# Score maxima in nine units of 512 keys in place of twelve of 384

## The chip, the cores and the metric

The kernel runs on one core of a Trainium2 chip. That core has a matrix engine (TensorE, PE in the profile, with its weight loads listed apart as PEld), a vector engine (VectorE, DVE), a scalar engine (ScalarE, ACT), GpSimd (POOL) and SyncE (SP), which issues the transfers here. The metric is the device time of one execution in microseconds, median of three runs.

## The reference

Attention over pooled queries, and behind it a feed-forward layer with g = h − tanh(h) in the middle:

```python
q_pool = q.reshape(B, H, S // 2, 2, D).mean(axis=3)          # B=8, H=8, S=1152, D=64
scores = np.matmul(q_pool, k.transpose(0, 1, 3, 2)) / np.sqrt(D)
scores = scores - np.max(scores, axis=-1, keepdims=True)
attn = np.exp(scores)
attn = attn / (np.sum(attn, axis=-1, keepdims=True) + 1e-09)
x = np.matmul(attn, v)            # then laid out as 4608 tokens x 512
h = x @ w_in                      # 512 x 2048
out = (h - np.tanh(h)) @ w_out    # 2048 x 512
```

All of it is float32. Each head has 576 pooled queries and 1152 keys. The part that the change touches is `np.max(scores, axis=-1)`.

## The kernel before

Two heads form a pair and lie in the two halves of the 128 partitions (64 rows each), so that two matmuls with 64 rows of contraction, one for each head, run side by side. There are 32 pairs. For each pair the program makes these stages, in this order on PE:

- **Scores.** 18 places, two halves of the queries (288 each) by nine tiles of 128 keys. At each place (`scores`) PE makes a transposed score tile of both heads, keys on partitions, by four pairs of matmuls of 288 columns: high by high part, high by low, low by high, and a row of maxima (`m_row` with `sel`) that subtracts each query's maximum. ACT takes the exponential out of the PSUM buffer into a tile `p`, and POOL adds the `p` tiles up for the sums.
- **P·V.** 18 places again; at each PE multiplies one `p` tile with `v` (float32). When a half is done ACT copies the result out (`pv_out`).
- **Sums** of the exponentials, by matmuls with ones, and ACT copies them out (`s_s`).

The maxima are wanted per query before a pair's scores begin, so they are computed one pair ahead. `max_part(pi, i)` is one step of this: it takes a PSUM buffer, PE writes untransposed scores (queries on partitions) of the high parts of `q` and `k` of both heads into it, and DVE reduces them to one maximum per query and head (`mx`). The 576 queries are four tiles of 128 and a last one of 64; the two heads' last tiles share one operand, `q_last`. Steps 0 to 11 are four tiles by three thirds of the keys (CH = 384), steps 12 and 13 the last tile. `max_row` then combines the three partial maxima of each query (`nm`), transposes them and sends them through DRAM (`m_dram`) into the row `m_row`.

Where a step stands is written out by hand. A table `at` holds, for each pair and place, what is to be done behind that place's scores or P·V step. Every engine is wrapped so that its instructions keep the order in which the program names them. For the pair after the current one, steps 0 to 11 stand behind places 1, 2, 4, 5, 7, 8, 10, 11, 13, 14, 16 and 17 of the scores, `max_row` behind place 17; steps 12 and 13 of a pair stand two pairs ahead, behind the sums. DVE has other work in the P·V stage: the query sums (`raw`), the low parts (`kq_l`) and, in most pairs, a quarter of it at a time, the conversion of the feed-forward weights (tiles `w_t`, `w_hl`).

All these users of PSUM share one ring of four buffers of two banks each:

```python
ring = new("ring", 4, space=PSUM)
def psum():
    return ring.tile([P, 2, 512], F32, name="ps")
```

A buffer is handed out in the order of the calls: score, maximum step, P·V result and sums alike. Whoever takes a buffer waits until the fourth call before it has been read out, by ACT (scores, `o_s`, `s_s`) or by DVE (maxima). Head 0 writes the first bank of a buffer, head 1 the second.

After the last pair the feed-forward stage follows, from about 825 us on, in its own PSUM buffers.

The profile gives nearly all instructions the line of the helper that keeps the order (L37), so they are told apart by tiles: `mx<-ps` is a maximum's reduction, `ps<-kq_h` with 384 columns its matmul, with 288 columns the first of a score's four pairs.

Of the kernel before, what the change touches and what calls it, by code (L numbers as in the profile page):

```python
# [12 lines left out]
ALU = mybir.AluOpType  # L13
AX = mybir.AxisListType
# [32 lines left out]
def attention_ffn_kernel(  # L47
# [16 lines left out]
    P = 128  # L64
    B, NP, _, _, SQ = q.shape
    S = k.shape[-1]
# [4 lines left out]
    CH = S // 3  # L71
# [5 lines left out]
    pe, act, dve, pool, sp = (InOrder(tc, e) for e in (nc.tensor, nc.scalar, nc.vector, nc.gpsimd, nc.sync))  # L77
# [32 lines left out]
    class X:  # L110
# [25 lines left out]
        def high(self, c):  # L136
            act.activation(self.h[:, c], self.r[c], AF.Copy)

        def low(self, eng, c):
            eng.tensor_tensor(self.l[:, c], self.r[c], self.h[:, c].bitcast(F32), op=ALU.subtract)  # L140
# [14 lines left out]
    with ExitStack() as actx:  # L155
# [6 lines left out]
        op = new("op", 2)  # L162
# [17 lines left out]
        def rows(t, h):  # L180
            return t[h * D:h * D + D]

        def psum():
            return ring.tile([P, 2, 512], F32, name="ps")
# [42 lines left out]
            sp.dma_start(w.v, v[w.b, w.hp])  # L227


        order = [(t, c) for t in range(4) for c in range(3)] + [(4, 0), (4, 2)]  # L230

        def max_part(pi, i):

            w = pairs[pi]
            t, c = order[i]
            q0 = t * P
            ps = psum()
            if t < 4:
                for h in range(2):
                    pe.matmul(ps[:, h, 0:CH], rows(w.hi, h)[:, q0:q0 + P], rows(w.hi, h)[:, SQ + c * CH:SQ + (c + 1) * CH],  # L240
                              start=True, stop=True)
                dve.tensor_reduce(w.mx[:, t, c], ps[:, :, 0:CH], axis=AX.X, op=ALU.max)
            else:
                n = min(2, 3 - c)
                for a in range(n):
                    pe.matmul(ps[:, a, 0:CH], q_last[pi % 2], w.hi[:, SQ + (c + a) * CH:SQ + (c + a + 1) * CH],
                              start=True, stop=True)
                dve.tensor_reduce(w.mx[:, 4, c // 2, 0:n], ps[:, 0:n, 0:CH], axis=AX.X, op=ALU.max)
# [147 lines left out]
        def add(pi, place, f, *args):  # L396
            at.setdefault((pi, place), []).append(lambda: f(*args))

        for pi in range(1, n_pair):
            for i in range(12):  # L400
                add(pi - 1, i // 2 * 3 + 1 + i % 2, max_part, pi, i)
            if pi >= 2:
                for i in range(12, 14):
                    add(pi - 2, 2 * NS, max_part, pi, i)
            add(pi - 1, NS - 1, max_row, pi)
        for pi in range(n_pair):
# [36 lines left out]
        load_v(0)  # L443
        query_sums(0)
        high(0, 2)
        for i in range(9):
            max_part(0, i)
        max_row(0, 0, 3)
        low(0)
        for i in range(9, 14):  # L450
            max_part(0, i)
        max_row(0, 3, 4)
        query_sums(1)
        high(1)
        for i in range(12, 14):
            max_part(1, i)
        blocks[0].load()

# [4 lines left out]
        for pi in range(n_pair):  # L463
            w = pairs[pi]
            ps = [Half(), Half()]
# [101 lines left out]
    for ci in range(len(chunks)):  # L567
        c = Chunk()
# [8 lines left out]
        for f in range(NF):  # L577
            n = ci * NF + f
# [71 lines left out]
```

## Time and profile before

| | |
|---|---|
| time, median of 3 runs | 1634.74 us (1633.24 to 1636.42) |
| the profiled execution's own time | 1633.7 us |
| its span | 1631.9 us |
| mean granted TensorE clock | 0.996 |
| PE busy | 1586.2 us, 97% of the span |
| DVE busy | 1280.5 us, 78% |
| ACT busy | 938.5 us, 58% |
| first and last maximum reduction start | 8.0 and 793.8 us |

A group row gives line, engine, operation, output and input tiles with shapes and the number of instructions; behind the bar the time that they were busy, the mean duration of one in ns, then the idle time of the engine ahead of them and who ended it. A timeline row gives start and length in us, then the same names; instructions of one kind that follow each other are merged into a row ("x2"), and in brackets stands the idle time before and what ended it. A window row gives the stretch and its length, then busy time and count of PE, PEld, DVE, ACT and POOL, the granted clock, the share of the DMA engines and GB/s. The chain of waits goes back from the last instruction to what released each one.

### The profile page before, as it was taken

The numbers are of one execution on the slowest core, as the hardware profiler recorded it, in microseconds if no ns is written. First come the engines' busy times: TensorE is split into PE (matmuls) and PEld (weight loads), VectorE is DVE, ScalarE is ACT, GpSimd is POOL, SyncE is SP. The second block draws the span as 40 slices with busy tenths as digits, with TensorE's granted clock in tenths as the row PEclk, the third lists the DMA queues.
The fourth block names the chain that finished last, engine by engine and source line by source line (L and its number), as shares of the span: only waits on it lengthen the run. The fifth ranks groups of instructions, "written<-read, shape, count | busy, mean of one in ns | idle before, by whom it ended". The sixth has DMA issues, their size and how long they took to land.

```text
span 1631.9 us, 30673 instructions
## 1 busy us (share of the span) xinstructions
PE 1586.2 (97%) x12012; PEld 1228.4 (75%) x12012; DVE 1280.5 (78%) x1621; ACT 938.5 (58%) x1584; POOL 1113.3 (68%) x749
## 2 busy tenths in 40 slices
PE   5999999999999999999999999999999999999998
PEld 4777676776776776777768888888888888888886
DVE  6788888898889898969447777777777777777776
ACT  3565565565655656656535656555555656555554
POOL 3777786776767767778756666666757675666654
PEclk9999999999999999999999999999999999999999
DMA  4335444344453554333471101001010101020000
GB/s 169 107 119 197 167 150 182 133 183 162 155 214 135 200 182 160 131 123 100 152 310 34 65 7 48 31 7 65 13 65 14 65 14 65 13 65 10 30 1 26
DMA packets 79602, 166.15 MB, mean 102 GB/s; under 512 B 11874, under 2 KB 38498, under 8 KB 77410
## 3 DMA queue, kind: packets, MB, share of 16 engines
q1 hardware_dynamic: 79458, 164.20, 28.3%
q8 instruction: 94, 1.54, 0.4%
q14 instruction: 50, 0.41, 0.1%
HBM read 126.12 MB, written 38.04 MB: 101 GB/s over the span
## 4 chain that ended last, share of the span: by engine, by line
PE 83%; DVE 11%; DMA 2%; issue 2%; ACT 2%; POOL 0%; SPq 0%; POOLq 0%; DVEq 0%; ACTq 0%
PE ps L37 35%; PE ps_h L37 24%; PE ps_o L37 24%; DVE mx L37 3%; DVE w_t L37 3%; DVE kq_l L37 1%; DVE w_hl L37 1%; DMA wi_dram<-w_hl 1%; DVE raw L37 1%; ACT w_t L37 1%; DMA m_dram<-tr 0%; SPq L37 0%; DMA q<-in_q_dram 0%; ACT q_last L37 0%; POOL sum L37 0%
## 5 line engine op out<-in xcount | busy, mean ns | idle before, releaser
L37 DVE TENSOR_REDUCE mx<-ps 128x2 f32<-128x768 f32 x448 | 396.6, 924 | 86.9 <-PE ps L37 85.0
L37 POOL TENSOR_TENSOR sum<-p,p 128x576 f32<-128x576 f32 x192 | 300.6, 1566 | 196.7 <-ACT p L37 196.5
L37 ACT ACTIVATE p<-ps 128x576 f32<-128x576 f32 x576 | 353.2, 653 | 112.1 <-PE ps L37 93.7
L37 POOL TENSOR_SCALAR g_m<-g_u 128x512 uint8<-128x512 f32 (+1 forms) x145 | 250.6, 1728 | 197.6 <-ACT g_u L37 182.5
L37 POOL TENSOR_TENSOR sum<-sum,p 128x576 f32<-128x576 f32 x192 | 301.1, 1568 | 29.2 <-ACT p L37 15.1
L37 PE MATMUL ps<-kq_h 64*128 64x288 f32 (+1 forms) x1920 | 289.3, 345 | 28.0 <-DVE mx L37 17.6
L37 PE MATMUL ps<-p,v 128*64 128x288 f32 x2304 | 286.4, 407 | 0.1
L37 DVE SCALAR_TENSOR_TENSOR ps_w<-g_u,ps_h 128x512 f32<-128x512 f32 (+1 forms) x145 | 100.4, 693 | 191.3 <-ACT g_t L37 191.2
L37 PEld LDWEIGHTS ps<-p,v 128*64 128x64 f32 x2304 | 162.6, 137 | 114.4 <-ACT p L37 6.9
L37 POOL TENSOR_TENSOR g_lo<-g_s,g_hi 128x512 fp32r<-128x512 f32 (+1 forms) x145 | 186.6, 1287 | 89.5 <-ACT g_hi L37 89.5
L37 PE MATMUL ps_o<-w,g_hi 128*128 128x512 f32 x792 | 244.5, 390 | 1.0 <-ACT g_hi L37 1.0
L37 PEld LDWEIGHTS ps<-kq_h 64*128 64x128 f32 x1920 | 181.3, 187 | 80.8 <-DVE mx L37 33.0
L37 ACT ACTIVATE g_u<-ps_h 128x512 f32<-128x512 f32 (+1 forms) x145 | 85.8, 591 | 244.0 <-PE ps_h L37 242.3
L37 PE MATMUL ps_h<-x_h,w 128*128 128x512 f32 (+1 forms) x800 | 214.8, 390 | 0.0
L37 ACT ACTIVATE g_s<-g_u,pc 128x512 f32<-128x512 f32 x290 | 193.2, 714 | 11.3
L37 PEld LDWEIGHTS ps_h<-x_h,w 128*128 128x128 f32 x800 | 149.6, 188 | 32.4
L37 PEld LDWEIGHTS ps_o<-w,g_hi 128*128 128x128 f32 x792 | 148.5, 188 | 33.6 <-ACT g_hi L37 1.4
L37 PE MATMUL ps<-kq_l,kq_h 64*128 64x288 f32 x1152 | 171.8, 295 | 0.0
L37 PE MATMUL ps<-kq_h,kq_l 64*128 64x288 f32 x1152 | 171.5, 294 | 0.0
L37 PE MATMUL ps<-m_row,sel 64*128 64x288 f32 x1152 | 171.2, 293 | 0.0
L37 PE MATMUL ps_o<-w,g_lo 128*128 128x512 f32 x396 | 154.8, 391 | 0.6 <-POOL g_lo L37 0.5
L37 DVE COPY_PREDICATED g_s<-g_m,g_t 128x512 f32<-128x512 uint8 (+1 forms) x145 | 108.4, 748 | 15.0
(92 smaller groups left out, 2368.3 us busy)
## 6 DMA issues: line engine op xcount, KB each, us to landing
raw<-in_k_dram SPq DMA_DIRECT2D x32, 576.0 KB
q<-in_q_dram SPq DMA_DIRECT2D x32, 576.0 KB
v<-in_v_dram SPq DMA_DIRECT2D x32, 576.0 KB
x_dram<-o_s SPq DMA_DIRECT2D x32, 288.0 KB
x_l<-x_dram SPq DMA_DIRECT2D x9, 1024.0 KB
out_dram<-o_f SPq DMA_DIRECT2D x36, 256.0 KB
w_raw<-in_w_in_dram SPq DMA_DIRECT2D x8, 1024.0 KB
w_off<-in_w_in_dram SPq DMA_DIRECT2D x8, 1024.0 KB
```

The lines of the kernel that those rows point to most:

```text
L37: i = f(*args, **kwargs)
```

## The change

The four full query tiles have 4 × 1152 = 4608 columns of keys. They are cut into nine units of 512 columns that run on from one tile into the next. Units 0, 1, 3, 5, 7 and 8 lie in one tile; unit 2 has 128 columns of tile 0 and 384 of tile 1, unit 4 256 and 256 of tiles 1 and 2, unit 6 384 and 128 of tiles 2 and 3. A unit takes one buffer of the ring and fills both its banks. A unit in one tile has two matmuls of 512 columns (one a head) and one reduction of 2 × 512 elements; one that crosses has four matmuls and two reductions. Each tile still gets three partial maxima. The units stand behind the places 1, 3, 5, ... 17; the last tile's two steps keep their place, behind the sums two pairs ahead. In the opening, ahead of pair 0, seven units stand where nine steps stood ahead of the first `max_row`.

```diff
@@ -227,20 +227,38 @@
             sp.dma_start(w.v, v[w.b, w.hp])
 
 
-        order = [(t, c) for t in range(4) for c in range(3)] + [(4, 0), (4, 2)]
+
+
+        units, n_part = [], {}
+        for u in range(0, 4 * S, 512):
+            units.append([])
+            left = 512
+            while left:
+                t, k0 = divmod(u, S)
+                n = min(S - k0, left)
+                units[-1].append((t, n_part.setdefault(t, 0), k0, n))
+                n_part[t] += 1
+                u, left = u + n, left - n
+        assert set(n_part.values()) == {3}
+        NU = len(units)
 
         def max_part(pi, i):
 
             w = pairs[pi]
-            t, c = order[i]
-            q0 = t * P
             ps = psum()
-            if t < 4:
-                for h in range(2):
-                    pe.matmul(ps[:, h, 0:CH], rows(w.hi, h)[:, q0:q0 + P], rows(w.hi, h)[:, SQ + c * CH:SQ + (c + 1) * CH],
-                              start=True, stop=True)
-                dve.tensor_reduce(w.mx[:, t, c], ps[:, :, 0:CH], axis=AX.X, op=ALU.max)
+            if i < NU:
+                at_ = 0
+                for t, c, k0, n in units[i]:
+                    for h in range(2):
+                        pe.matmul(ps[:, h, at_:at_ + n], rows(w.hi, h)[:, t * P:(t + 1) * P], rows(w.hi, h)[:, SQ + k0:SQ + k0 + n],
+                                  start=True, stop=True)
+                    at_ += n
+                at_ = 0
+                for t, c, k0, n in units[i]:
+                    dve.tensor_reduce(w.mx[:, t, c], ps[:, :, at_:at_ + n], axis=AX.X, op=ALU.max)
+                    at_ += n
             else:
+                c = 2 * (i - NU)
                 n = min(2, 3 - c)
                 for a in range(n):
                     pe.matmul(ps[:, a, 0:CH], q_last[pi % 2], w.hi[:, SQ + (c + a) * CH:SQ + (c + a + 1) * CH],
@@ -397,10 +415,10 @@
             at.setdefault((pi, place), []).append(lambda: f(*args))
 
         for pi in range(1, n_pair):
-            for i in range(12):
-                add(pi - 1, i // 2 * 3 + 1 + i % 2, max_part, pi, i)
+            for i in range(NU):
+                add(pi - 1, 2 * i + 1, max_part, pi, i)
             if pi >= 2:
-                for i in range(12, 14):
+                for i in range(NU, NU + 2):
                     add(pi - 2, 2 * NS, max_part, pi, i)
             add(pi - 1, NS - 1, max_row, pi)
         for pi in range(n_pair):
@@ -443,16 +461,16 @@
         load_v(0)
         query_sums(0)
         high(0, 2)
-        for i in range(9):
+        for i in range(7):
             max_part(0, i)
         max_row(0, 0, 3)
         low(0)
-        for i in range(9, 14):
+        for i in range(7, NU + 2):
             max_part(0, i)
         max_row(0, 3, 4)
         query_sums(1)
         high(1)
-        for i in range(12, 14):
+        for i in range(NU, NU + 2):
             max_part(1, i)
         blocks[0].load()
```

On PE, in the score stage, the ring's users follow each other as score, step, score, score, step before. A piece of it, a step and the two scores behind it, with the semaphores that each waits for (`Activation` is ACT, `Activation` and `DVE` free a ring buffer):

```order
L37 MATMUL ps<-kq_h 128x384 [waits Activation_49]
L37 MATMUL ps<-kq_h 128x384
L37 MATMUL ps<-kq_h 128x288 [waits Activation_49]
L37 MATMUL ps<-kq_h 128x288
L37 MATMUL ps<-kq_l,kq_h 128x288 x2
L37 MATMUL ps<-kq_h,kq_l 128x288 x2
L37 MATMUL ps<-m_row_119,sel 128x288 x2
L37 MATMUL ps<-kq_h 128x288 [waits DVE_49]
L37 MATMUL ps<-kq_h 128x288
L37 MATMUL ps<-kq_l,kq_h 128x288 x2
L37 MATMUL ps<-kq_h,kq_l 128x288 x2
L37 MATMUL ps<-m_row_119,sel 128x288 x2
```

The same with the change, at unit 1:

```order
L37 MATMUL ps<-kq_h 128x512 [waits Activation_49]
L37 MATMUL ps<-kq_h 128x512
L37 MATMUL ps<-kq_h 128x288 [waits DVE_49]
L37 MATMUL ps<-kq_h 128x288
L37 MATMUL ps<-kq_l,kq_h 128x288 x2
L37 MATMUL ps<-kq_h,kq_l 128x288 x2
L37 MATMUL ps<-m_row_119,sel 128x288 x2
L37 MATMUL ps<-kq_h 128x288 [waits Activation_49]
L37 MATMUL ps<-kq_h 128x288
L37 MATMUL ps<-kq_l,kq_h 128x288 x2
L37 MATMUL ps<-kq_h,kq_l 128x288 x2
L37 MATMUL ps<-m_row_119,sel 128x288 x2
```

Now every third user is a step, and the score right behind a step takes the buffer of the step before the last one; the score behind that one takes a buffer that ACT frees. Further on, past unit 3, the score that takes the buffer of unit 2 (a unit in two parts) waits for two semaphores, DVE's and PE's own:

```order
L37 MATMUL ps<-kq_h 128x512 [waits Activation_49]
L37 MATMUL ps<-kq_h 128x512
L37 MATMUL ps<-kq_h 128x288 [waits DVE_49,PE_49]
L37 MATMUL ps<-kq_h 128x288
L37 MATMUL ps<-kq_l,kq_h 128x288 x2
```

On DVE, behind the two steps of the last tile and up to the row maxima, before:

```order
L37 TENSOR_REDUCE mx<-ps 128x2 [waits PE_49]
L37 TENSOR_REDUCE mx<-ps 128x1 [waits PE_49]
L37 TENSOR_REDUCE mx<-ps 128x2 [waits PE_49] x12
L37 TENSOR_REDUCE nm_121<-mx 128x4x2 [waits DVE_49]
L37 TENSOR_REDUCE nm_121<-mx 128x1
```

and with the change:

```order
L37 TENSOR_REDUCE mx<-ps 128x2 [waits PE_49]
L37 TENSOR_REDUCE mx<-ps 128x1 [waits PE_49]
L37 TENSOR_REDUCE mx<-ps 128x2 [waits PE_49] x3
L37 TENSOR_REDUCE mx<-ps 128x2
L37 TENSOR_REDUCE mx<-ps 128x2 [waits PE_49] x2
L37 TENSOR_REDUCE mx<-ps 128x2
L37 TENSOR_REDUCE mx<-ps 128x2 [waits PE_49] x2
L37 TENSOR_REDUCE mx<-ps 128x2
L37 TENSOR_REDUCE mx<-ps 128x2 [waits PE_49] x2
L37 TENSOR_REDUCE nm_120<-mx 128x4x2 [waits DVE_49]
L37 TENSOR_REDUCE nm_120<-mx 128x1
```

There are twelve reductions in both. In units 2, 4 and 6 the first of the two waits for PE, at a count that stands behind all four matmuls of the unit, and the second waits for nothing.

## The prediction

> **What bounds the kernel now.** I read the page's totals and chain first, then the windows of two pairs, then the timelines of PE, DVE and ACT in them.
>
> ```profile
> span 1631.9 us, 30673 instructions
> PE 1586.2 (97%) x12012; PEld 1228.4 (75%) x12012; DVE 1280.5 (78%) x1621; ACT 938.5 (58%) x1584; POOL 1113.3 (68%) x749
> PE 83%; DVE 11%; DMA 2%; issue 2%; ACT 2%; POOL 0%; SPq 0%; POOLq 0%; DVEq 0%; ACTq 0%
> ```
>
> PE carries the chain, DVE a ninth of it. But a busy PE is not a PE at its peak, so the score stage has to be opened. A pair has 18 places of scores, with the next pair's maxima between them, and then P·V and the sums. The windows below are the score stage and the rest for pair 27 (first two) and for pair 24.
>
> ```profile
> 705.49:717.90 12.41, 12.41 (x166) 11.01 (x162) 10.60 (x13) 10.42 (x18) 10.44 (x8) 1.00 0.17 51
> 717.90:729.61 11.71, 11.71 (x108) 6.74 (x108) 6.43 (x8) 3.92 (x7) 8.52 (x5) 1.00 0.38 123
> 630.34:644.62 14.28, 12.71 (x166) 11.08 (x162) 12.56 (x15) 10.42 (x17) 10.94 (x8) 1.00 0.77 296
> 644.62:656.32 11.70, 11.70 (x107) 6.75 (x107) 11.53 (x14) 5.11 (x8) 9.02 (x5) 1.00 0.31 103
> ```
>
> The second half takes 11.70 us in both (PE works through). The score stage differs: 12.41 us in a clean pair, 14.28 in one that DVE (third busy number, 12.56 and 11.53) reaches late, because it still converts weights. Of the 31 pairs that compute maxima, 12 have a stage of 12.41 to 12.45 us (pair 27 stands for them) and 19 a longer one (pair 24 stands for them).
>
> The clean stage, PE:
>
> ```profile
> 705.61 0.29 PE L37 MATMUL ps<-kq_h 64*128 64x288 f32 x2
> 705.75 0.30 PE L37 MATMUL ps<-kq_l,kq_h 64*128 64x288 f32 x2
> ...
> 706.14 0.65 PE L37 MATMUL ps<-kq_h 64*128 64x384 f32 x4
> 706.63 0.30 PE L37 MATMUL ps<-kq_l,kq_h 64*128 64x288 f32 x2
> ...
> 707.03 0.50 PE L37 MATMUL ps<-kq_h 64*128 64x384 f32 x4
> 707.36 0.29 PE L37 MATMUL ps<-kq_l,kq_h 64*128 64x288 f32 x2
> ...
> 707.76 0.29 PE L37 MATMUL ps<-kq_h 64*128 64x288 f32 x2
> ...
> 708.28 0.53 PE L37 MATMUL ps<-kq_h 64*128 64x384 f32 x4
> ...
> 710.44 0.50 PE L37 MATMUL ps<-kq_h 64*128 64x384 f32 x4
> ...
> 717.90 0.71 PE L37 MATMUL ps<-p,v 128*64 128x288 f32 x4
> ```
>
> The same stretch on DVE, and one ACT row and two weight loads:
>
> ```profile
> 704.91 1.42 DVE L37 TENSOR_REDUCE mx<-ps 128x2 f32<-128x768 f32 x2 [5.20 <-PE ps L37]
> 708.66 1.82 DVE L37 TENSOR_REDUCE mx<-ps 128x2 f32<-128x768 f32 x2 [0.30 <-PE ps L37]
> 710.81 1.82 DVE L37 TENSOR_REDUCE mx<-ps 128x2 f32<-128x768 f32 x2 [0.33 <-PE ps L37]
> ...
> 717.27 1.82 DVE L37 TENSOR_REDUCE mx<-ps 128x2 f32<-128x768 f32 x2 [0.33 <-PE ps L37]
> ```
>
> ```profile
> 712.33 1.90 ACT L37 ACTIVATE p<-ps 128x576 f32<-128x576 f32 x3 [0.24 <-PE ps L37]
> ```
>
> ```profile
> 711.42 0.19 PEld L37 LDWEIGHTS ps<-kq_h 64*128 64x128 f32 x2 [0.20 <-ACT p L37]
> 711.53 0.19 PEld L37 LDWEIGHTS ps<-kq_l,kq_h 64*128 64x128 f32 x2
> ```
>
> Three places repeat every 2.15 us (708.66 to 710.81). PE waits 0.20 us there for an exponential, ACT idles 0.24 of it and DVE 0.33: three engines nearly level, tied by the ring of four score buffers. So one place costs 0.715 us, two cost 1.43.
>
> **Sizes, from these rows.** One pair of matmuls of 288 columns takes 0.13 us (705.61 to 705.75). A score is 0.525 (705.61 to 706.14 is 0.53; 707.76 to 708.28 is 0.52), two are 1.05. A maximum of 384 columns takes PE 0.33 − 0.13 = 0.20 (707.03 to 707.36 holds it and a score's first pair). By the 288 columns in 0.13, another 128 add some 0.055, so a unit of 512 takes 0.25. Entry, from a unit's start on PE to its reduction: 708.28 to 708.66 and 710.44 to 710.81, mean 0.375; for 512 columns 0.43. Exit, from a reduction's end to the score it frees: the two at 704.91 end at 706.33, the freed score's second pair starts at 706.63, its first 0.13 before: 0.17. The reductions' own times:
>
> ```profile
> L37 DVE TENSOR_REDUCE mx<-ps 128x2 f32<-128x768 f32 x416 | 381.7, 953 | 86.9 <-PE ps L37 85.0
> ...
> L37 DVE TENSOR_REDUCE mx<-ps 128x1 f32<-128x384 f32 x32 | 17.5, 547 | 0.0
> ```
>
> (953 − 547) / 384 = 1.057 ns an element; so 1024 elements 1.22 us, 512 0.68, 256 0.41. Two of 953 back to back take 1.82, an overlap of 0.09.
>
> **The change, part by part.** Per pair it keeps 24 matmuls, 4608 columns a head, and 12 reductions with the same elements: 12 × 953 = 11.44 us before; 6 × 1.22 + 2 × (0.41 + 0.95) + 2 × 0.68 = 11.4 after. PE's own work stays too. ACT is untouched. What goes is three turns of the ring per pair (12 units become 9), and with them the ACT loop of 2.15 us: in the new order a score waits for an exponential of three scores earlier, which ends in time at 0.63 us each (1.90 / 3). What comes is a buffer that is held longer by DVE, and a pattern of period three (score, score, unit) on a ring of four: the first score of each block of two places takes the buffer of the unit two units back. That gives a loop over two blocks:
>
> whole unit: entry 0.43 + reduction 1.22 + exit 0.17 + two scores 1.05 = 2.87 us;
> unit in two parts: the order shows one wait for all four matmuls ahead of its first reduction, none ahead of the second. Entry 0.46 (for 128 + 384 the extra pair costs at least a weight load's spacing, 711.42 to 711.53, 0.11, so 0.48; 0.44 for 256 + 256), two reductions 1.36 − 0.09 = 1.28 (1.27 or 1.28 by either split), exit 0.17, scores 1.05, and a second wait on PE that the order shows in front of the freed score. No row prices it; bounds 0 and 0.11 (a load's spacing); I take 0.05, the middle. Sum 3.01.
>
> PE's own work in two blocks is 2 × (1.05 + 0.25) = 2.60, so this loop decides, not PE. The parted units are 2, 4 and 6, all of one parity, so they stand in one chain.
>
> Clean pair, b1 = start of the second block = 706.63 − 0.13 = 706.50. Unit 0 starts at 706.14 as now; b2 = 706.14 + 0.43 + 1.22 + 0.17 = 707.96, that is b1 + 1.46. Three parted loops: b8 = b1 + 1.46 + 9.03 = b1 + 10.49. Two scores and the last unit, 1.30: P·V starts at b1 + 11.79. Now it starts at 717.90, b1 + 11.40. **+0.39 us.** The last reduction ends at b8 + 1.05 + 0.43 + 1.22 = b1 + 13.19 = 719.69, against 717.27 + 1.82 = 719.09: +0.60.
>
> Late pair, DVE first, then PE:
>
> ```profile
> 631.69 3.44 DVE L37 TENSOR_REDUCE mx<-ps 128x2 f32<-128x768 f32 x4
> ...
> 643.99 1.82 DVE L37 TENSOR_REDUCE mx<-ps 128x2 f32<-128x768 f32 x2 [0.33 <-PE ps L37]
> ```
>
> ```profile
> 632.70 0.87 PE L37 MATMUL ps<-kq_h 64*128 64x384 f32 x4 [1.54 <-DVE mx L37]
> 633.40 0.30 PE L37 MATMUL ps<-kq_l,kq_h 64*128 64x288 f32 x2
> ```
>
> ```profile
> 644.62 0.71 PE L37 MATMUL ps<-p,v 128*64 128x288 f32 x4
> ```
>
> DVE starts at D = 631.69 with the two last-tile maxima of the pair after next. Unit 0 starts at D + 0.95 + 0.17 = D + 1.12; b2 = D + 1.12 + 1.82 = D + 2.94; b8 = D + 11.97; P·V at D + 13.27 against 644.62 = D + 12.93: +0.34. Last reduction ends at D + 11.97 + 2.70 = D + 14.67 against 645.81 = D + 14.12: +0.55. Behind it on DVE stand the row maxima, the next query sums and low parts and the weight steps, the same list as before, and then the next pair's reductions:
>
> ```profile
> 654.71 2.14 DVE L37 TENSOR_SCALAR w_t<-w_t 128x1024 f32<-128x1024 f32 x3
> 656.76 3.44 DVE L37 TENSOR_REDUCE mx<-ps 128x2 f32<-128x768 f32 x4
> ```
>
> So where DVE is late the whole 0.55 is handed on; after a clean pair the delay is 0.60 − 0.39 = 0.21 behind P·V, and 0.21 + 0.34 = 0.55 again. In clean pairs DVE's idle time (5.20 us before 704.91) covers that 0.21; without that cover they too would cost 0.55.
>
> Ahead of the loop DVE reduces pair 0's maxima with the same element count and the same instructions: nothing. The feed-forward stage is not touched: nothing. Sum: 19 × 0.55 + 12 × 0.39 = 10.4 + 4.7 = **+15.1 us** on the profiled execution's 1633.7 us (span 1631.9): 1648.8. The median of the runs shown, 1634.74, lies 1 us above that execution; I predict 1649, between what either would give.
>
> The Trainium skill ("Perfetto Trace Analysis", section "Matmuls" under "Optimizing Tensor Performance") says that larger matmuls are more efficient when possible, and that groups should rotate through PSUM banks so that evacuation overlaps the next group. By its first half 512 columns should beat 384; by the trace that half would be worth nothing while PE is not the limit, and it is the second half that this change strains.
>
> **Rivals.**
> *PE bound.* If the freed buffers were no limit, blocks would run at PE's 1.30 us: from b1 eight blocks, 10.4 against 11.40, −1.0 × 31 = −31 us, 1603. For it: three fewer turns, and the idle 0.20 us per 2.15. Against: it needs a unit's buffer back 1.55 us after its start (0.25 + 1.05 + 0.25), and entry, reduction and exit are 1.82. It decides only if a 1024 reduction took under 0.95 us, as long as one of 768. This is where the skill's first half would lead. 6%.
> *The parted units cost no more than whole ones*, DVE starting on the first part while PE makes the second. Then the other parity decides: P·V at b1 + 4 × 2.87 = 11.48, +0.08 clean, and D + 1.58 + 11.48 = 13.06, +0.13 late: 19 × 0.13 + 12 × 0.08 = 3.4 us, 1637. Against: the single wait. 14%.
> *The second wait or DVE's restart costs more*, 0.1 more in each of three loops: 0.3 × 31 = 9 us on top, 1658. For it: PE cannot load ahead while it stands in that wait. 12%.
> *The change does not reach the chip as written*: the order shows nine units of up to 512 columns, so under 1%, no separate case.
>
> **How the numbers follow.** Forecast 68%, rivals 6, 14 and 12. What this kernel's measurement tells from no change is about 0.2%, 3.3 us, so 1637 lies astride it: half of that 14% is "same", and I add 2% for loops that all come out at 2.85 us, four of which are the 11.40 of now. Faster 7% (PE bound, with 1% for a partial gain), same 9%, slower 84%. Range: the bounds of the second wait (0 and 0.11) move the sum by 3 × 0.05 × 31 = 5 us either way, entry and exit 0.02 each way in four loops another 3; the lower end reaches toward the parted-unit rival: 1639 to 1658.
>
> **What would show it.** Right: DVE's reductions of 1024 at 1.22 us; PE loads waiting on "DVE mx" at every second block in place of "ACT p", 0.2 to 0.4 us each; clean score stages of 12.8 us and late ones some 0.55 longer than now; P·V's first load released by DVE. Wrong: stages at or under 12.41 us, no wait on "DVE mx" inside clean pairs, or waits that still name "ACT p"; two reductions of one unit starting before its last matmul would be the second rival.

## The result, and the profile after

The changed kernel takes 1653.43 us (median of four runs, 1650.67 to 1654.92) against 1634.74 us before. The ratio is 1.0118, with a 95% interval of 1.0101 to 1.0134: slower, by 18.7 us. The forecast was 1649 us, with a range of 1639 to 1658. The profiled execution took 1653.2 us; its span is 1651.4 us against 1631.9, so the two traces differ by 19.5 us, and this is the sum to be explained.

The page's totals and its chain, of the kernel after:

```profile
span 1651.4 us, 30769 instructions
PE 1590.5 (96%) x12012; PEld 1225.2 (74%) x12012; DVE 1280.8 (78%) x1621; ACT 928.8 (56%) x1584; POOL 1100.3 (67%) x749
PE 81%; DVE 13%; issue 2%; DMA 2%; ACT 1%; POOLq 0%; POOL 0%; SPq 0%; DVEq 0%; ACTq 0%
```

The engines do what they did: as many matmuls and as many reductions, PE's busy time 4 us longer and DVE's as long. DVE's share of the chain went from 11 to 13%. The time went into waits, as these rows of the waits (engine and tile that wait, who ends it; us in total, times, longest) show:

```profile
PEld ps L37 <- PE ps L37: 42.2, 94, 1.0
PEld ps L37 <- DVE mx L37: 38.0, 77, 3.9
PE ps L37 <- DVE mx L37: 29.2, 51, 3.7
```

Before, PE's loads waited 28.2 us, 135 times, for the exponentials ("PEld ps <- ACT p"). Of that row one wait of 0.2 us is left. The first row here is new, with three waits per pair: a score that takes the buffer of a parted unit waits for DVE and for PE itself, and the view puts the wait under PE.

The windows of three score stages of the kernel after: a clean pair (27), a pair that DVE reaches late (24), and pair 7, whose stage took 13.06 us before. Columns as in the prediction; the third busy number is DVE's, and behind POOL's stands the granted clock.

```profile
724.73:737.77 13.04, 12.63 (x166) 10.94 (x162) 10.85 (x13) 10.14 (x18) 11.06 (x8) 1.00 0.18 59
647.26:661.84 14.58, 12.97 (x167) 10.98 (x163) 12.46 (x15) 10.15 (x18) 11.51 (x9) 1.00 0.75 289
205.52:224.00 18.48, 14.29 (x167) 12.53 (x163) 14.86 (x17) 10.24 (x18) 11.79 (x9) 0.91 0.23 91
```

Pair 27 went from 12.41 to 13.04 us, pair 24 from 14.28 to 14.58, pair 7 from 13.06 to 18.48. Laid out in this way for all 31 score stages that compute maxima (sums of their lengths, each rounded, from the first `m_row` matmul to the first of P·V):

| pairs | before, us | after, us | difference, us |
|---|---|---|---|
| the 12 clean ones | 149.0 | 156.5 | +7.5 |
| 7, 16, 21 and 25 | 54.2 | 66.5 | +12.3 |
| 15 and 18 | 31.6 | 29.2 | −2.3 |
| the other 13 | 180.1 | 183.3 | +3.2 |
| all else (opening, P·V and sums, feed-forward) | | | −1.0 |

The second half of a pair takes 11.70 us as before. So the loss stands in the score stages, as forecast, but it lies unevenly: four pairs carry 12.3 of 19.5 us.

**The clean stage in detail.** PE in pair 27 of the kernel after; the first row holds unit 0 and the first matmuls of the score behind it, the rows of `kq_l,kq_h` are the second pair of a score that waited for a reduction:

```profile
725.39 0.66 PE L37 MATMUL ps<-kq_h 64*128 64x512 f32 x4
725.88 0.30 PE L37 MATMUL ps<-kq_l,kq_h 64*128 64x288 f32 x2
...
727.34 0.30 PE L37 MATMUL ps<-kq_l,kq_h 64*128 64x288 f32 x2
...
730.40 0.33 PE L37 MATMUL ps<-kq_l,kq_h 64*128 64x288 f32 x2
...
733.44 0.32 PE L37 MATMUL ps<-kq_l,kq_h 64*128 64x288 f32 x2
...
736.48 0.33 PE L37 MATMUL ps<-kq_l,kq_h 64*128 64x288 f32 x2
...
737.77 1.19 PE L37 MATMUL ps<-p,v 128*64 128x288 f32 x8
```

The loop over two blocks can be read off: 725.88 to 727.34 is b1 to b2, 1.46 us. Then three loops through a parted unit, 3.06, 3.04 and 3.04, together 9.14. From 736.48 to P·V are 1.29 us, and with the first score's own pair, 0.13 earlier, 1.42. DVE in the same stretch, and two of PE's loads:

```profile
725.83 1.22 DVE L37 TENSOR_REDUCE mx<-ps 128x2 f32<-128x1024 f32 x1 [0.24 <-PE ps L37]
727.26 1.23 DVE L37 TENSOR_REDUCE mx<-ps 128x2 f32<-128x1024 f32 x1 [0.20 <-PE ps L37]
728.76 2.60 DVE L37 TENSOR_REDUCE mx<-ps 128x2 f32<-128x256 f32 x3 [0.28 <-PE ps L37]
731.80 2.52 DVE L37 TENSOR_REDUCE mx<-ps 128x2 f32<-128x512 f32 x3 [0.44 <-PE ps L37]
```

```profile
727.11 0.19 PEld L37 LDWEIGHTS ps<-kq_h 64*128 64x128 f32 x2 [0.24 <-DVE mx L37]
...
730.17 0.21 PEld L37 LDWEIGHTS ps<-kq_h 64*128 64x128 f32 x2 [0.41 <-PE ps L37]
```

Read the rows of DVE as follows: a row of three is a parted unit's two reductions and the whole unit behind it. The whole unit's reduction ends at 725.83 + 1.22 = 727.05, and the freed score starts at 727.34 − 0.13 = 727.21, so the exit is 0.16. Behind a parted unit PE's load waits 0.41 instead of 0.24.

### The profile page after: what moved, and what is told of

Same layout as the page of the kernel before. It is cut to its first block, busy times and chain, and to the rows that moved or that the text cites. A ratio compares the mean times of both kernels' runs of the same rounds, so it can differ in the third digit from the quotient of the medians.

```text
span 1651.4 us, 30769 instructions
## 1 busy us (share of the span) xinstructions
PE 1590.5 (96%) x12012; PEld 1225.2 (74%) x12012; DVE 1280.8 (78%) x1621; ACT 928.8 (56%) x1584; POOL 1100.3 (67%) x749
## 3 DMA queue, kind: packets, MB, share of 16 engines
q8 instruction: 94, 1.54, 0.4%
## 4 chain that ended last, share of the span: by engine, by line
PE 81%; DVE 13%; issue 2%; DMA 2%; ACT 1%; POOLq 0%; POOL 0%; SPq 0%; DVEq 0%; ACTq 0%
PE ps L37 34%; PE ps_h L37 24%; PE ps_o L37 23%; DVE mx L37 5%; DVE w_t L37 2%; DVE w_hl L37 2%; DVE raw L37 1%; DVE kq_l L37 1%; DMA wi_dram<-w_hl 1%; ACT w_t L37 1%; DMA wo_dram<-w_hl 0%; DMA q<-in_q_dram 0%; ACT q_last L37 0%; DVE nm L37 0%; DVE ps_w L37 0%
## 5 line engine op out<-in xcount | busy, mean ns | idle before, releaser
L37 DVE TENSOR_REDUCE mx<-ps 128x2 f32<-128x1024 f32 (+3 forms) x448 | 403.1, 926 | 104.6 <-PE ps L37 99.2
L37 POOL TENSOR_TENSOR sum<-p,p 128x576 f32<-128x576 f32 x192 | 291.9, 1520 | 227.0 <-ACT p L37 227.0
L37 ACT ACTIVATE p<-ps 128x576 f32<-128x576 f32 x576 | 343.6, 652 | 141.1 <-PE ps L37 136.2
L37 PE MATMUL ps<-kq_h 64*128 64x288 f32 (+4 forms) x1920 | 303.2, 341 | 42.7 <-DVE mx L37 28.9
L37 POOL TENSOR_TENSOR sum<-sum,p 128x576 f32<-128x576 f32 x192 | 296.3, 1543 | 33.0 <-ACT p L37 19.1
L37 PEld LDWEIGHTS ps<-kq_h 64*128 64x128 f32 x1920 | 186.3, 188 | 101.1 <-PE ps L37 41.5
L37 PE MATMUL ps<-kq_l,kq_h 64*128 64x288 f32 x1152 | 180.4, 295 | 0.0
L37 PE MATMUL ps<-kq_h,kq_l 64*128 64x288 f32 x1152 | 179.9, 294 | 0.0
L37 PE MATMUL ps<-m_row,sel 64*128 64x288 f32 x1152 | 179.7, 293 | 0.0
```

The lines of the kernel that those rows point to most:

```text
L37: i = f(*args, **kwargs)
```

## The experiments

The theory was that of the prediction: a unit's buffer comes back too late for a ring of four (hold time), and the parted units add two costs of their own (a second reduction's restart, a second wait on PE). The rivals in the first four runs: 512 columns are dear by themselves, whatever DVE does; or parted units cost no more than whole ones.

**1. Shorter reductions.** After, with each unit's reduction over three quarters of its columns; all matmuls stay.

```diff
-                    dve.tensor_reduce(w.mx[:, t, c], ps[:, :, at_:at_ + n], axis=AX.X, op=ALU.max)
+                    dve.tensor_reduce(w.mx[:, t, c], ps[:, :, at_:at_ + n * 3 // 4], axis=AX.X, op=ALU.max)
```

> The changed kernel, with every reduction reading only the first three quarters of its columns (a quarter of the keys is left out of the maxima); matmuls, buffers, places and waits stay. Held-buffer theory (a unit's buffer is freed by DVE too late, loop over two blocks): whole loop 1.06 + 0.445 + 0.95 + 0.15 = 2.61 us instead of 2.88, loop of a parted unit 2.78 instead of 3.05. From the second block to P.V 1.31 + 3 x 2.78 + 1.42 = 11.1 instead of 12.0, so a clean score stage of 12.1 us (now 13.04), DVE waits of PE down to 0.1 us or so in a block. Rival (the wide matmuls or the pattern on PE and ACT make the stage long, DVE's length does not matter as long as it idles): 12.9 to 13.1.

Measured: 1631.49 us, ratio to the kernel before 0.9992 (0.9981 to 1.0003). The clean stage (pair 27's window):

```profile
702.19:714.26 12.07, 12.07 (x167) 10.99 (x163) 8.71 (x13) 10.16 (x18) 10.09 (x8) 1.00 0.17 51
```

12.07 us instead of 13.04, with PE busy throughout. PE's matmuls are those of the changed kernel, so its extra time in a clean pair is not PE's, but the time for which DVE holds the buffer.

**2 and 3. Nine whole units, of 512 and of 384 columns.** The two differ only in the size of a unit. Both leave keys out of the maxima, and `max_row` combines two partial maxima of a query in place of three.

```diff
-        units, n_part = [], {}
...
+        units = [[(t, c, c * 512, 512)] for t, c in ((0, 0), (0, 1), (0, 2), (1, 0), (1, 1), (2, 0), (2, 1), (3, 0), (3, 1))]
+        units[2] = [(0, 2, S - 512, 512)]
...
```

> The changed kernel with nine units of 512 that each lie in one query tile (two matmuls, one reduction): the first 1024 keys of each tile, and one unit of tile 0 over its last 512 that is not used; the last 128 keys are left out of the maxima. Held-buffer theory: no parted loops and no second wait, all loops 2.88: 1.45 + 3 x 2.88 + 1.42 = 11.5 from the second block, and 4 x 2.88 + 0.1 = 11.6 by the other parity: clean stage 12.6 us (now 13.04). Rival (parted units cost no more than whole ones, all of the loss is size): 13.0.

> As the kernel with nine whole units, but of 384 columns: pattern and places of the change, size of the step before; the last 384 keys of each tile are left out of the maxima. Held-buffer theory: loop 1.06 + 0.375 + 0.95 + 0.15 = 2.54, PE's own two blocks 2 x (1.06 + 0.20) = 2.52: blocks of 1.27, 1.3 + 3 x 2.54 + 1.06 + 0.27 = 10.3 from the second block, clean stage 11.3 us, below the 12.41 of the kernel before; whole kernel some 30 us under the changed one. Rival (the pattern score, score, unit is itself the loss): 12.4 or longer.

Measured: 1637.88 us with 512 columns, ratio 1.0021 (1.0008 to 1.0034); 1620.84 us with 384, ratio 0.9924 (0.9905 to 0.9944). The clean stages, 512 first:

```profile
708.66:721.20 12.54, 12.54 (x160) 10.55 (x157) 10.64 (x10) 10.15 (x18) 10.56 (x8) 1.00 0.16 50
```

```profile
696.09:707.34 11.25, 11.25 (x161) 10.54 (x157) 8.51 (x10) 10.09 (x17) 9.35 (x7) 1.00 0.20 60
```

With the same nine turns of the ring at the same places, no unit parted, 512 columns cost 1.29 us more than 384 in this pair and in three others (1, 2 and 28). In the other eight of the twelve clean pairs the gap is 0.2 to 0.7, since the stage of the kernel with 384 columns takes 11.8 to 12.3 us there. Nine whole units of 512 take 0.13 more than the twelve of 384 before (12.41). So what the three saved turns bring is more than eaten up by the size.

**4. One reduction per unit, all maxima kept.** A reduction now leaves the maximum of each 128 keys, 8 values in place of 2 or 4, so a tile's border falls between values and a parted unit needs one instruction. `max_row` reduces 18 values a query instead of 6.

```diff
-                at_ = 0
-                for t, c, k0, n in units[i]:
-                    dve.tensor_reduce(w.mx[:, t, c], ps[:, :, at_:at_ + n], axis=AX.X, op=ALU.max)
-                    at_ += n
+                dve.tensor_reduce(w.mx[:, 8 * i:8 * i + 8].rearrange("p (a h) -> p h a", h=2), ps.rearrange("p h (a n) -> p h a n", n=P),
+                                  axis=AX.X, op=ALU.max)
...
```

> The changed kernel with one reduction a unit in all nine units: maxima of 128 keys each, four a head and unit (36 instead of 12 partial maxima of a head, which the row maxima then combine); matmuls, buffers and places stay, the second wait on PE goes. Held-buffer theory: a parted loop is a whole one plus 0.03 of entry, 2.91: 1.45 + 3 x 2.91 + 1.42 = 11.6, clean stage 12.65 us (now 13.04), whole kernel some 10 us under the changed one and 5 to 10 over the one before. Rival (parted units cost no more than whole ones): clean stage 13.0, time as the changed kernel. If short runs of 128 elements cost DVE more, its reductions are longer than 1.22 us and the stage is longer by twice that a loop.

Measured: 1637.28 us, ratio 1.0033 (1.0018 to 1.0048). The group of its reductions and the clean stage:

```profile
L37 DVE TENSOR_REDUCE mx<-ps 128x8 f32<-128x1024 f32 x288 | 351.6, 1224 | 64.1 <-PE ps L37 57.1
```

```profile
707.17:719.76 12.59, 12.59 (x166) 10.91 (x162) 10.66 (x10) 10.16 (x18) 10.61 (x8) 1.00 0.16 50
```

The reduction takes 1224 ns, as long as with two values a row, and the row "PEld ps <- PE ps" is gone from the waits. DVE in the clean stage (each row a unit of the loop and the one behind it):

```profile
711.20 2.58 DVE L37 TENSOR_REDUCE mx<-ps 128x8 f32<-128x1024 f32 x2 [0.30 <-PE ps L37]
714.09 2.58 DVE L37 TENSOR_REDUCE mx<-ps 128x8 f32<-128x1024 f32 x2 [0.30 <-PE ps L37]
716.99 2.58 DVE L37 TENSOR_REDUCE mx<-ps 128x8 f32<-128x1024 f32 x2 [0.32 <-PE ps L37]
```

The loop is 2.89 us (711.20 to 714.09), against 3.05 through a parted unit. So the parted units cost 0.45 of the 0.63 us that a clean pair loses, and of the ratio's 1.18% they carry 0.85 (1.0118 against 1.0033), some 14 us. The loops explain a part of this: 12 × 0.45 = 5.4 us in the clean pairs. But pairs 7, 16, 21 and 25 lose only 3.3 us in this run, 9.0 less than after. What happens in those four was the next question, and with it how a late pair works at all.

**5. The late pairs.** In the traces of these runs one thing does not fit the prediction: DVE's lateness (its first last-tile reduction against the start of the score stage) should have grown by 0.21 us, and in pair 24 it fell from 1.35 to 1.09. The weight work in that pair, DVE and GpSimd, before:

```profile
624.76 3.29 DVE L37 TENSOR_SCALAR w_t<-w_t 128x1024 f32<-128x1024 f32 x3 [1.47 <-ACT w_t L37]
```

```profile
624.64 1.40 POOL L37 TENSOR_TENSOR sum<-sum,p 128x576 f32<-128x576 f32 x1
```

and after:

```profile
642.54 2.15 DVE L37 TENSOR_SCALAR w_t<-w_t 128x1024 f32<-128x1024 f32 x3 [1.49 <-ACT w_t L37]
```

```profile
640.57 1.76 POOL L37 TENSOR_TENSOR sum<-sum,p 128x576 f32<-128x576 f32 x1
```

The same three instructions take 3.29 us where a GpSimd addition runs when they start, and 2.15 where it has ended 0.21 us earlier. The groups say the same: the first of the three, a clamp of which there are 16, takes 1249 ns on average before and 689 after.

The next run takes that addition away from the kernel before: the last one of each pair. Its sums leave out one `p` tile.

```diff
-            elif r == 2:
+            elif r == 2 and (half, k) != (1, 2):
                 pool.tensor_tensor(ps.sum[k], ps.sum[k], ps[kt], op=ALU.add)
```

> The kernel before without GpSimd's last add of each pair (the last p tile is left out of the sums of the second half). Theory on GpSimd: its adds end 1.4 us earlier, about when they end in the changed kernel relative to DVE, so the clamp's first instruction falls from 1249 ns to about 700 and the eight pairs start 0.2 instead of 1.35 us late: some 9 us off. Rival (not GpSimd): 1249 ns, no change in DVE's part.

Measured: 1619.68 us, ratio 0.9916 (0.9891 to 0.9942).

```profile
L37 DVE TENSOR_SCALAR w_t<-w_t 128x1024 f32<-128x1024 f32 x16 | 11.0, 690 | 11.9 <-ACT w_t L37 11.9
```

The clamp falls to 690 ns and the lateness in pairs 3, 6, 12, 15, 18 and 24 from 1.35 to 0.25 us. That a GpSimd addition lengthens DVE's instruction is shown. The gain was larger than expected (13 us on the spans, not 9); 2.7 of it came from pairs 15 and 18, which have no half clock here (below).

**6 and 7. Another place for the weight step.** If overlap is the matter, the step may be moved: behind place 9 of P·V in place of 6, in the kernel before and in the kernel after.

```diff
-                if pi >= 2 and place in (3, 6, 11, 15) and work:
+                if pi >= 2 and place in (3, 9, 11, 15) and work:
```

> The kernel before (twelve steps of 384), with one edit away from the maxima: the second weight step of a pair's P.V stage stands behind place 9 instead of 6, so behind the low parts kq_l. In the pairs in which the weight clamp falls there, DVE now waits 1.5 us for ACT and then takes 1.83 us for the clamp's first instruction while GpSimd adds, against 0.69 when GpSimd is idle. Theory (DVE's elementwise instructions in these stages are lengthened by GpSimd's adds, and that sets how late a pair starts): mean of the clamp's first instruction from 1249 ns to about 700, the eight pairs that start 1.35 us late start about 0 late, stage 14.3 to 13.0: 8 x 1.2 = 10 us off the kernel, 1624. Rival (the length comes from the operands or from ACT's order, and kq_l moves into GpSimd's adds for as much): no change.

> The changed kernel with the weight step moved behind place 9 as well. Here GpSimd has finished its adds when the clamp comes (its first instruction already takes 689 ns on average), so by the theory on GpSimd the clamp gains nothing, only ACT's wait of 1.5 us goes, and kq_l moves 1.5 us ahead into the adds (up to 3.2 us instead of 1.95): eight pairs less late by 0 to 0.5, 0 to 4 us off the changed kernel. If the gain is as large as in the kernel before (10 us), GpSimd is not what differs.

Measured: before with place 9: 1630.38 us, ratio 0.998 (0.9966 to 0.9994); after with place 9: 1651.24 us, 1.011 (1.0076 to 1.0143). The first was a miss. DVE's wait of 11.9 us for ACT went, but the order brought the low parts in front, and now these meet the additions:

```profile
622.02 3.20 DVE L37 TENSOR_TENSOR kq_l<-raw,kq_h 128x1728 fp32r<-128x1728 f32 x1
625.14 3.35 DVE L37 TENSOR_SCALAR w_t<-w_t 128x1024 f32<-128x1024 f32 x3
```

In the kernel before that instruction took 1.95 us in pair 24 (at 627.96), here 3.20, and the weight step behind it is no shorter than it was. Lateness fell by 0.1 us only. GpSimd's addition beside the two was held as well:

```profile
623.48 3.00 POOL L37 TENSOR_TENSOR sum<-sum,p 128x576 f32<-128x576 f32 x1
```

On the changed kernel the edit did what was expected, next to nothing: 1.011 against 1.0118, well inside the interval. The six pairs that were late by 1.1 us are late by 0.9, and the four pairs take 19.2, 18.5, 14.7 and 14.8 us (7, 16, 21 and 25).

**8. The changed kernel once more**, unedited, to see whether the four pairs are chance.

> The changed kernel once more, unedited, for a second profile. Held-buffer theory: the twelve clean pairs again at 13.04 us, late pairs with 13.5 us from DVE's start to P.V. The six pairs that were longer by 1.4 to 5.4 us in one of the two profiles (half clock, or DVE waiting for a weight store): if chance, other pairs or other amounts; if a property of the change, the same pairs, 7 with 18.5 us above all.

Measured: 1654.56 us, ratio 1.0123 (1.0101 to 1.0144); pairs 7, 16, 21 and 25 take 19.2, 17.2, 16.5 and 15.0 us. The same four came back. Pairs 7, 16 and 25 are long in run 7 as well, so they go with the change; pair 21 is not, and its excess hangs on the clock alone (see the last section). The chain of waits of the kernel after ahead of pair 7 (start, length, what), and the chain of the kernel before at the same place:

```profile
197.07 2.37 DVE w_hl L37
199.44 0.02 issue
199.46 5.66 DMA wi_dram<-w_hl
...
207.30 1.83 DVE w_t L37
```

```profile
195.62 4.02 DMA wi_dram<-w_hl
```

DVE wants to write `w_hl` for the next weights while the last ones are still on their way to DRAM. That transfer takes 5.66 us and took 4.02. DVE and PE behind it, after:

```profile
205.24 0.69 DVE L37 TENSOR_SCALAR w_hl<-w_off 128x1024 int32<-128x1024 int32 x1 [2.72 <-DMA wi_dram<-w_hl]
205.85 3.28 DVE L37 TENSOR_SCALAR w_t<-w_t 128x1024 f32<-128x1024 f32 x3
209.05 2.77 DVE L37 TENSOR_REDUCE mx<-ps 128x2 f32<-128x768 f32 x3
```

```profile
210.05 0.86 PE L37 MATMUL ps<-kq_h 64*128 64x512 f32 x4 [3.71 <-DVE mx L37]
```

```profile
210.80:214.20 3.40, 3.40 (x30) 3.31 (x30) 2.17 (x2) 1.43 (x3) 1.42 (x1) 0.50 0.00 0
```

Pair 7's lateness grew by 3.40 us, from 0.13 to 3.53. Its parts: the transfer 1.64; the third instruction on `w_t`, which now runs into the next pair's first addition, 1.83 − 0.69 = 1.14; the last reduction, which ends 0.15 later behind P·V; and the issue of the transfer, 0.48 later behind that reduction, since the query sums met an addition too (0.72 us before, 1.37 after). Sum 3.41. PE then waits 3.71 us, and the granted clock (0.50 in the last row) is at half for 3.40 us, which makes the stage another 1.45 longer (first last-tile reduction to P·V, 14.95 against 13.50 in undisturbed late pairs). Pairs 16 and 21 have the half clock as well, pair 25 a wait of 1.12 us for the transfer of the other weights.

**9 and 10. Later loads.** A guess at why the transfer takes longer: the loads of the next keys and queries run beside it. They were put behind place 16 of P·V in place of 12, in the kernel after, and in the kernel before together with place 9.

```diff
-                add(max(pi - 3, 0), NS + 12 if pi > 2 else 0, load, pi)
+                add(max(pi - 3, 0), NS + 16 if pi > 2 else 0, load, pi)
```

> The changed kernel with the loads of k and q (tiles raw and q2) issued behind place 16 of the P.V stage instead of 12; nothing else. In pairs 7 and 16 of the changed kernel DVE waits 2.7 and 2.2 us for a weight store that takes 5.7 us to land (4.0 in the kernel before), with these loads issued 3 us behind it, PE then waits 3.7 us and its clock is halved for one or two windows. If the loads are what slows the store: store 4.0 to 4.3 us, wait 1.0 to 1.3 us, stages of pairs 7 and 16 from 18.5-19.2 and 16.8-17.2 us to 13.5-15, whole kernel 6 to 9 us under the changed one. Clean pairs stay at 13.04. Rival (the store is slow by itself once it starts later, for example behind the other store half): both stages stay within 1 us.

> The kernel before with two edits away from the maxima: the weight step behind place 9 (as in the run before) and the loads of k and q behind place 16. If the loads slow the stores, the 5 to 7 us in which DVE waits for stores shrink to 2 to 3 and the kernel is 3 to 5 us under the run with place 9 alone, 1626; if not, 1630 as there.

Measured: 1653.38 us, ratio 1.0106 (1.008 to 1.0131), and 1632.59 us, ratio 0.9974 (0.9959 to 0.9989). The edit did not reach what it was meant to move: the loads wait for their buffer, which the low parts free, and started 8.7 us behind P·V in either order. DVE still waited 2.5 and 2.6 us for the transfer ahead of pairs 7 and 16. Pair 7's stage fell to 15.66 us all the same, because the third instruction on `w_t` just misses the addition and no half clock follows, and pair 16's rose to 18.32. So this run decides nothing on the transfer. The second kernel is no better than place 9 alone.

The traces say more on why the transfer takes 5.66 us. These rows are of the DMA queues in the kernel after, ahead of pair 7; the first two are the stretch 199.4 to 202.5 us, the last is 202.6 to 203.4:

```profile
DMA packets 1975, 1.01 MB, mean 327 GB/s; under 512 B 25, under 2 KB 1974, under 8 KB 1974
...
q8 instruction: 1, 0.02, 1.8%
...
DMA packets 35, 0.02 MB, mean 22 GB/s; under 512 B 1, under 2 KB 35, under 8 KB 35
```

At 200.50 us a packet of 16 KB comes in on the queue that the profile lists as `instruction`, and takes 0.88 us. Before, such a packet came at 199.13, when the transfer was all but done. Of the transfer's packets 95% have begun 3.08 us after the first one (2.91 before), but the last one begins only after 5.32 us (3.14 before). What is left runs at 22 GB/s, near a sixteenth of 327, as if one of the 16 DMA engines were behind. The twelve profiles of this document have 24 such transfers, ahead of pairs 7 and 16. In twelve of them an instruction packet begins within 1.2 us of the first packet, and the last packet begins after 4.3 to 5.3 us; in the other twelve none begins before 2.8 us, and it is 3.13 to 3.15 us each time. The packets of the loads begin 3.4 us or more behind the transfer's first. So the loads are not what makes it long, and the instruction packet very likely is; no run moved that packet by itself, so this is read from traces and not tested.

Of the kernels that compute all the maxima and all the sums, only the two with place 9 and the twelve old units come out under the kernel before, by 0.2 to 0.3%. No form of the nine units of 512 does.

## Why the prediction was right, and where it was not

**The bound: right.** The loop through a buffer that DVE holds sets the clean stage, not PE: waits on the exponentials vanished, waits on the reductions took their place, and with reductions a quarter shorter (run 1) the loss was gone.

**Sizes of the loop: a little short.** Whole loop: predicted 2.87, measured 2.89 (run 4). Reductions: 1.22 predicted, 1224 ns measured; a parted unit's two 1.28 predicted, 1.29 measured. Parted loop: 3.01 predicted, 3.05 measured. The exit behind a whole unit is 0.16 and behind a parted one 0.22, and 0.22 is what the prediction had for exit and second wait together (0.17 + 0.05). The 0.04 come from the entries (0.50, 0.46 and 0.47 against 0.46) and, 0.01 each, from reductions and scores. Three such loops give 9.14 in place of 9.03.

**The tail: mis-sized.** "Two scores and the last unit, 1.30" took 1.42. The unit of 512 was sized at 0.25 by columns; from its start to P·V go 0.36 us (737.41 to 737.77; a unit of 384 takes 0.27 there before, not 0.20). P·V's load shows that time as issue. It isn't released by DVE, as "What would show it" had it. Loops 0.11 and tail 0.12 make the clean pair +0.63 us in place of +0.39, and the late one's D to P·V 13.50 in place of 13.27.

**Late pairs: one step wrong.** "Behind it on DVE stand ... the same list as before ... so where DVE is late the whole 0.55 is handed on." The same instructions, but not the same time: the list from the last reduction to the next D took 11.89 us before in pair 24 (619.80 to 631.69) and 11.45 after (636.89 to 648.34). The reduction's end moved some 0.15 later behind P·V, and GpSimd's last addition moved the other way: it ended 7.43 us behind P·V before, 6.77 after (in a slower stage GpSimd lags less behind the exponentials; this is argued, not shown). The first instruction of DVE's weight step, held by that addition before, runs free after (1.83 and 0.70 us). The query sums went the other way, since they meet an earlier addition, before and after:

```profile
620.35 1.10 DVE L37 TENSOR_TENSOR raw<-q 128x576 f32<-128x576 f32 x1
```

```profile
637.43 1.78 DVE L37 TENSOR_TENSOR raw<-q 128x576 f32<-128x576 f32 x1
```

−1.13 and +0.68 make up the difference. So pair 24 lost 0.30 and not 0.55: +0.56 in D to P·V, −0.26 in lateness. Run 5 shows the mechanism from the other side.

The Trainium skill ("SBUF — State Buffer", section "Who interferes with whom") says that VectorE in its two-port modes and GpSimd lock each other out of a shared port pair for a whole instruction. The two traces agree: before, the addition ends at 624.64 + 1.40 = 626.04 and DVE's first instruction, begun at 624.76, at 626.59; ahead of pair 7 another addition ends at 208.58 and DVE's instruction at 207.30 + 1.83 = 209.13. Both end 0.55 us behind the addition, which is nearly the 0.69 of an undisturbed one.

**Not foreseen: the four pairs.** The prediction moved DVE's work by half a microsecond and asked only what stands behind it on DVE and PE. It did not ask what else each instruction meets at its new time: a transfer that has not landed (pairs 7 and 16, and 25), an addition of the next pair (7), and a wait on PE that halves the clock (7, 16, 21). These cost 12.3 us; pairs 15 and 18, which had the half clock before, gave 2.3 back. Where the half clock falls is no property of the change (last section): run 10 has it in pairs 6, 9, 15 and 18, run 6 in 10 and 21. The kernel before was profiled once, so those 2.3 us may be chance.

**The sum.** Forecast +15.1: 4.7 from clean pairs, 10.4 from late ones. Measured +19.5 in the profiled executions: 7.5 clean, 13.1 late (the table's three rows, before rounding), −1.0 elsewhere. For the late pairs two errors of opposite sign cancelled in part: most of them lost far less than 0.55, and four lost 3.1 on average. That the total came out 4 us from the forecast is in part luck.

**The rivals.** *PE bound* fell: the reduction of 1024 takes 1.22 us. *Parted units no dearer* was priced at +3.4 us. Run 4, in which a parted unit has one reduction and costs no more than a whole one, is 0.33% over the kernel before, some 5 us. Its size was near and its condition false: the first reduction of a parted unit starts behind all four matmuls (728.26 to 728.76 for unit 2). *Second wait dearer* was right in sign, 0.04 a loop in place of 0.1, but not in its cause.

## What to carry to other kernels

In a ring of buffers with several users, a unit's price is not its matmuls, but how long its buffer is held (entry, reduction, exit) against the time until its turn comes again; a larger unit saves turns and lengthens the hold, and only what is measured against the ring's length decides. When a reduction has to be split for a border in the data, let one instruction write more partial results: 8 values a row cost the same 1224 ns as 2, and saved 14 of the 18.7 us (9 of them in the four pairs, where much hangs on what DVE's work happens to meet). And a delay on an engine isn't a number to be handed on: list what every instruction behind it will meet at its new time, the transfers that free its tiles and the engine that shares its memory port first of all.

## What the hardware did that was not expected

- A DVE instruction of 0.69 us takes 1.83 beside a GpSimd addition of 1.40, and either side can be the one that is held: with place 9 an addition took 3.00.
- The exit behind a parted unit, where the score waits for two semaphores, is 0.22 us in place of 0.16. Run 4 takes away the second wait and the second reduction together and has 0.16, so which of the two costs the 0.06 is not shown.
- The transfer of the same weights took 4.02 us in one order and 5.66 in another; the long ones are those into which a packet of the instruction queue falls (runs 9 and 10).
- What brings the half clock isn't a long wait alone. In each trace the half clock begins on a grid of 3.413 us: at 406.70 and 481.79 us before (75.09 apart, 22 times 3.413), at 210.82, 442.92 and 572.63 after (232.10 and 129.71 apart, 68 and 38 times). It lasts one window of this grid each time here, and two (6.83 us) in pair 7 of run 8. Before, PE waited 1.54 us in pair 15 and again in pair 24. Only the first was followed by half the clock. Its row of PE, and the windows of the grid around the two waits (the first number behind the length is PE's busy time):

```profile
404.91 0.86 PE L37 MATMUL ps<-kq_h 64*128 64x384 f32 x4 [1.54 <-DVE mx L37]
```

```profile
403.29:406.70 3.41, 1.84 (x22) 1.51 (x22) 3.30 (x5) 1.28 (x3) 1.40 (x1) 1.00 0.70 202
406.70:410.11 3.41, 3.41 (x32) 3.41 (x30) 2.20 (x3) 2.17 (x4) 2.83 (x2) 0.50 1.00 420
...
628.57:631.98 3.41, 2.58 (x31) 1.64 (x23) 3.38 (x4) 1.60 (x3) 0.00 (x0) 1.00 0.02 5
631.98:635.39 3.41, 2.67 (x32) 2.31 (x34) 3.04 (x4) 1.28 (x3) 1.94 (x2) 1.00 0.87 317
```

Pair 15's wait lies inside one window, which PE spends idle for 1.57 us; pair 24's is cut by the border at 631.98 and leaves 0.83 and 0.74. Laid out in this way for all twelve traces (40 to 800 us, windows at full clock), 31 of the 32 windows in which PE idles for 1.54 us or more are followed by half the clock, none of the 588 with less than 1.42, and 4 of the 19 between. So the same wait costs half a clock or nothing, by where it falls on the grid.

The Trainium skill ("TensorE: Matmul & The Clock Gate", section "What's actually happening") has a free-running window of 3413 ns, which agrees with the grid measured, and asks for an idle window of that length; here some 1.5 us of idle time within one window were enough, and the measurement decides.
